# Transformer block on one core: the front part in turns of four max products and six projection products, with every second max product in a transpose bank

## The chip, the cores and the metric

The kernel runs on one core of a Trainium2 chip. The metric is the device time of one execution in microseconds (us), taken as the median over runs. The engines have short names here: PE is TensorE (PEld its weight loads), DVE is VectorE, ACT is ScalarE, POOL is GpSimd, SP is SyncE, which here only issues DMAs. Every engine works through its own queue in order. Where one needs what another makes, a semaphore holds it back, and everything behind it in its queue.

## The reference

One transformer block with modulation from a condition vector c, for 2048 rows of 512 numbers, in float32. The attention has 32 heads of size 16 that share one key and one value head.

```
sa, ca, ga, sb, cb, gb = silu(c) @ w_mod            # six rows of 512
h = layernorm(x) * (1 + ca) + sa
q, k, v = h @ wq, h @ wk, h @ wv                     # q: 32 heads x 16, k and v: one head of 16
p = softmax(q @ k.T / 4)                             # 32 heads, 2048 x 2048 each
x = x + ga * ((p @ v) @ wo)
h = layernorm(x) * (1 + cb) + sb
x = x + gb * (gelu(h @ w1 + b1) @ w2 + b2)           # 1376 hidden
```

## The kernel before

**Tiling.** The projections run in float32 precision: each operand is split in a high and a low part, and each product is three (`mm3`, L155 and after). Attention is cut into 64 units, each of 256 rows and four heads. A unit goes through two passes over the keys. The first makes scores only for their row maxima: *max products* `m` (PE, L512, 64 rows of the array, 512 keys each), of each of which DVE takes the maximum (L517, tile `mx`). With the maxima of a unit complete, `put_max` (L536) reduces them further (DVE, L565 and L566), POOL turns them into two rows, a high and a low part (`mt`, `mh`, `ml`), and `send` (L550) writes these into the query tile `qst` by DMA. Unit 0's four DMAs are issued half by SP and half by ACT. The second pass makes the scores again, now less their maximum (products `e`, L617), ACT takes the exps (L621), and PE multiplies them with the values (`acc`, L638).

**The front part.** Before the unit loop, the program normalises x in four blocks of 512 rows. For each block, `turn1` transposes it (tiles `tp`), `mod1` applies scale and shift (ACT, `h`, and its split `bigH`, `bigL`), and `kv_products` makes keys and values in `kps`: twelve products in four groups of three. From these, `kv_out` copies the high part of the keys into `ks` and the values into `vt` (ACT), `low_k` writes the low part (DVE), and `repeat_k` copies it to the other half of the array (ACT). `v_out` transposes the values (`vps`) and ACT copies them out (`va`, L420). Four groups of three query products (`qps`, "q 1") and the rows of the late modulation (`modl`, eight products at a time) come here too.

**Order.** The order is written by hand. `SLOTS` (L25) lists entries: a number of max products, then named jobs. The loop at L1353 goes through it; `chunk` makes the max products, alternately for the two halves of the array. After the list, the loop at L1376 makes max products up to a fixed count (two more), and `keep_warm` (L286) issues `WARM[3]` products on weights, whose result nobody reads (`idle`), in bank e2. Then the unit loop begins with its first `e`.

**Banks.** PE writes into PSUM banks. Max products turn through three (tag m), and a product waits until the reduce of the third product before it has read its bank. Three more, e0 to e2, are handed out in turn by `ebank()` to the transposes of the front part, and belong to the `e` products later. The projections have two others (x, v).

Of the kernel before, what the change touches and what calls it, by code (L numbers as in the profile page):

```python
# [8 lines left out]
F32 = mybir.dt.float32  # L9
F32R = mybir.dt.float32r  # L10
AF = mybir.ActivationFunctionType
ALU = mybir.AluOpType
AX = mybir.AxisListType

P = 128
# [7 lines left out]
LEAD_0 = 6  # L23
FIRST_MAX = ((0, 0), (1, 0), (0, 1), (1, 1), (0, 2), (0, 3), (1, 2), (1, 3))
SLOTS = ((2, "keys 1", "keys 1"), (2, "keys 1", "keys 1"), (2, "low 1", "heads 2"), (2, "heads 2", "k 1"), (1, "warm"), (1, "heads 2"), (2, "heads 2", "v 0"),  # L25
# [4 lines left out]
MAX_WAIT = (1, 4)  # L30
QBUFS = 4
PREP = 4
# [9 lines left out]
SOON = 6  # L42
GROUP = 4
NORM_WAIT = 6
WARM = (4, 16, 2, 5)
MOD_WAIT = 3
AHEAD = 4.5

# [1 line left out]
def raw(ap):  # L50
    return ap.bitcast(F32)
# [3 lines left out]
def adaln_mqa_mlp(  # L55
# [15 lines left out]
    nc = tc.nc  # L71
    _, S, D = x.shape
# [4 lines left out]
    BQ = 512  # L77
# [35 lines left out]
    ks = const.tile([P, S], F32R, name="ks")  # L113
# [13 lines left out]
    def ebank():  # L127
        turns[0] += 1
        return dict(tag=f"e{turns[0] % 3}", bufs=1)
# [30 lines left out]
    def mm3(ps, pairs, every=0, cost=0, begin=True, end=True):  # L160

        n, last = 0, 3 * len(pairs) - 1
        for wh, wl, xh, xl in pairs:
            for a, b_ in ((wh, xh), (wl, xh), (wh, xl)):
                nc.tensor.matmul(ps, a, b_, start=begin and n == 0, stop=end and n == last)  # L165
                n += 1
                if every and n % every == 0:
                    yield cost
# [50 lines left out]
    pro = pro_ctx.enter_context(tc.tile_pool(name="pro", bufs=1))  # L219
# [66 lines left out]
    def keep_warm(n, **place):  # L286

        for k in range(n):
            if k == 0 or not place:
                ps = psum.tile([P, BQ], F32, name=f"idle{len(idles)}", **(place or dict(tag="m", bufs=3)))  # L290
                idles.append(ps)
            nc.tensor.matmul(ps, wkH[:, 0, :], wkH.rearrange("p k n -> p (k n)"), start=True, stop=True)
# [64 lines left out]
    def stats1(b, between=None):  # L357
        mv, rs = ln_stats(xts[b], pro, QT, between)
        nm = pro.tile([P, QT], F32, name=f"nm{b}", tag="nm", bufs=2)
        if b:  # L360
            nc.gpsimd.tensor_tensor(out=nm, in0=mv[:, :, 0], in1=rs, op=ALU.mult)
            nc.gpsimd.tensor_scalar(out=nm, in0=nm, scalar1=-1.0, scalar2=0.0, op0=ALU.mult, op1=ALU.add)
        hts_stats[b] = mv, rs, nm

    def xhat1(b, eng):

        mv, rs, nm = hts_stats[b]
        xt = xts[b]
        for t in range(QT):
            if eng is nc.scalar:  # L370
                nc.scalar.activation(xt[:, t, :], xt[:, t, :], AF.Identity, scale=rs[:, t:t + 1], bias=nm[:, t:t + 1])
            else:
                eng.tensor_scalar(out=xt[:, t, :], in0=xt[:, t, :], scalar1=mv[:, t, 0:1], scalar2=rs[:, t:t + 1],
                                  op0=ALU.subtract, op1=ALU.mult)
            yield

    def turn1(b, d):
        ps = psum.tile([P, BQ], F32, name=f"tp{b}_{d}", **ebank())
        for t in range(QT):
            nc.tensor.transpose(ps[:, t * P:(t + 1) * P], xts[b][:, t, d * P:(d + 1) * P], ident)  # L380
        tps[b, d] = ps

    def mod1(b, d, eng_h, eng_l, between=None):
        hH, hL = hts[b]
        h32 = pro.tile([P, BQ], F32, name=f"h32_{b}_{d}", tag="h32", bufs=4)
        nc.scalar.activation(h32, tps.pop((b, d)), AF.Identity, scale=ca1[:, d:d + 1], bias=sa[:, d:d + 1])
        split(hH[:, d, :], hL[:, d, :], h32, eng_h, eng_l, between)

    kps = {}

    def kv_products(b):
        hH, hL = hts[b]
        kps[b] = psum.tile([P, BQ], F32, name=f"kps{b}", tag="x" if b == 3 else "v")
        return mm3(kps[b], [(wkH[:, k, :], wkL[:, k, :], hH[:, k, :], hL[:, k, :]) for k in range(KD)], 3)

    def kv_out(b):
        ps = kps[b]
        cols = slice(b * BQ, (b + 1) * BQ)
        vt = pro.tile([P, BQ], F32, name=f"vt{b}", tag="vt", bufs=2)
        for r in range(2):  # L400
            nc.scalar.copy(ks[64 * r:64 * r + 48, cols], ps[64 * r:64 * r + 48, :])
        nc.scalar.copy(vt[32:64, :], ps[32:64, :])
        vts[b] = vt

    def low_k(b):
        cols = slice(b * BQ, (b + 1) * BQ)
        nc.vector.tensor_tensor(out=ks[32:48, cols], in0=kps.pop(b)[32:48, :], in1=raw(ks[32:48, cols]), op=ALU.subtract)

    def repeat_k(b):
        cols = slice(b * BQ, (b + 1) * BQ)  # L410
        nc.scalar.copy(ks[96:112, cols], raw(ks[32:48, cols]))

    vts = {}

# [821 lines left out]
    first = [sum(size[:u]) for u in range(NU + 1)]  # L1236
    mp = Max()

    def chunk(n):
        for _ in range(n):  # L1240
            mp.step(mp.done % 2)

    act, dve, pool = nc.scalar, nc.vector, nc.gpsimd

    def k_products(b):
        for _ in kv_products(b):
            pass

    draining[0] = True
    late = [qproj_late(b, g) for b in range(2) for g in range(KD)]  # L1250
# [10 lines left out]
    def run(job, n=99):  # L1261
        for _ in range(n):
            if next(job, True):
                return

    def heads(b):

        for d in range(KD):
            turn1(b, d)
            mod1(b, d, pool if d == 1 else act, dve if b == 1 and d > 1 else pool)  # L1270
            if (b, d) == (2, KD - 1):
                load_mods(3)
            yield

    def keys(b):
        for i, _ in enumerate(kv_products(b)):
            if i == KD - 1:
                kv_out(b)
            yield

    def late_rows():
        for k in range(KD):
            if k == 0:
                mod_state["ps"] = psum.tile([P, D], F32, name="modl", tag="x")
            mod_rows(mod_state["ps"], k, mods_late[k])
            yield

    def q_group():
        for i in range(KD):
            next(projections[0])  # L1290
            if i == KD - 1:
                next(projections.pop(0))
            yield

    def warm():
        keep_warm(WARM[2], tag="x")
        yield

    def one(fn, *args):
        fn(*args)  # L1300
        yield
# [13 lines left out]
    turn1(0, 3)  # L1315
    keep_warm(WARM[0])
    mod1(0, 1, pool, dve, lambda: stats1(1))
# [3 lines left out]
    rows = xhat1(1, act)  # L1321
# [9 lines left out]
    run(rows)  # L1331
    run(keys(0))
    low_k(0)
    load_mods(0)
    load_mods(1)
    h1 = heads(1)
# [2 lines left out]
    def last_h(t):  # L1339
        if t == QT - 1:  # L1340
            run(h1)

    stats1(3, last_h)
    load_mods(2)
    repeat_k(0)
    run(xhat1(2, act))
    run(xhat1(3, pool))
    keep_warm(WARM[1])
    work = {"keys 1": keys(1), "heads 2": heads(2), "heads 3": heads(3), "q 1": q_group(), "keys 2": keys(2), "keys 3": keys(3),
            "v 0": one(v_out, 0), "v 1": one(v_out, 1), "v 2": one(v_out, 2), "v 3": one(v_out, 3), "rows": late_rows(),  # L1350
            "low 1": one(low_k, 1), "low 2": one(low_k, 2), "low 3": one(low_k, 3), "k 1": one(repeat_k, 1), "k 2": one(repeat_k, 2), "k 3": one(repeat_k, 3), "load": one(load_q, 2), "warm": warm(),
            "wq 1": one(prep_wq, 1), "wq 2": one(prep_wq, 2), "wq 3": one(prep_wq, 3)}
    for n, *names in SLOTS:  # L1353
        chunk(n)
        for name in names:
            next(work[name])
    assert 0 in placed and len(mods_late) == KD
    draining[0] = False
    nc.gpsimd.tensor_scalar(out=b1r, in0=b1c, scalar1=GELU_R, scalar2=0.0, op0=ALU.mult, op1=ALU.add)
# [16 lines left out]
    while mp.done < lead[0]:  # L1376
        chunk(1)
# [205 lines left out]
```

## Time and profile before

| | us |
|---|---|
| median of 3 runs | 1557.55 (1556.18 to 1559.13) |
| the profiled execution | 1555.99, span 1554.10 |
| heads-3 transposes end, projections of keys 2 begin on PE | 47.27 |
| L566 of unit 0 begins on DVE | 69.78 |
| first idle product | 73.75 |
| first `e` product | 75.14 |
| granted TensorE clock | 1.00 |

Rows of a timeline give start, duration, engine, line, operation, output and inputs, a count of like instructions in a row, and in brackets how long the engine stood before it and what ended this. Starts are counted from the span's beginning. Durations overlap on PE, whose products are pipelined, so what a product costs there is read from the distance of starts. Rows of the chain give start, length, engine and line. Rows by stretches give the stretch and its length, each engine's busy time, the granted clock and the DMA share.

### The profile page before, as it was taken

Reading aid. Unit: us, or ns where it says so; the run is one execution under the profiler, and the core shown is the slowest. Engines: PE = TensorE matmul, PEld = TensorE weight load, DVE = VectorE, ACT = ScalarE, POOL = GpSimd, SP = SyncE. Lnnn points to the kernel's source line nnn. Section 1 sums busy time; section 2 is a strip of 40 time slices with the busy share of each in tenths; the row PEclk is TensorE's granted clock in tenths of the full one; section 3 lists DMA queues with packets and bytes.
Section 4 is the critical chain, followed back from the end, with each engine's and each line's share of the span. In section 5 each row is a group of like instructions: output and inputs, shape, how many; then the busy total and the mean of one; then the engine's idle time right before and its main releaser. Section 6 shows DMA issues by size and latency. Waiting matters only on the chain.

```text
span 1554.1 us, 41556 instructions
## 1 busy us (share of the span) xinstructions
PE 1537.9 (99%) x16405; PEld 954.4 (61%) x16405; DVE 1398.3 (90%) x2488; ACT 1230.4 (79%) x2401; POOL 683.7 (44%) x1206
## 2 busy tenths in 40 slices
PE   7999999999999999999999999999999999999999
PEld 4455555567655665557655676556655676566658
DVE  7999999999999999999999999999999999999814
ACT  5577778788877887788877888788877888778874
POOL 5535432867422571246521563235711574046511
PEclk9999999999999999999999999999999999999999
DMA  7226412413030220303112120302212230203141
GB/s 240 102 89 199 151 57 81 130 51 97 18 105 26 72 68 28 103 19 109 33 51 79 56 87 16 111 26 88 68 30 73 60 101 25 87 28 99 48 150 48
DMA packets 84215, 120.85 MB, mean 78 GB/s; under 512 B 21342, under 2 KB 57438, under 8 KB 83764
## 3 DMA queue, kind: packets, MB, share of 16 engines
q1 hardware_dynamic: 84004, 118.18, 23.7%
q8 instruction: 130, 2.13, 0.6%
q14 instruction: 65, 0.53, 0.1%
q10 hardware_dynamic: 16, 0.00, 0.0%
HBM read 90.87 MB, written 26.74 MB: 76 GB/s over the span
## 4 chain that ended last, share of the span: by engine, by line
PE 86%; DVE 8%; issue 3%; POOL 2%; DMA 1%; ACT 0%; SPq 0%; POOLq 0%; DVEq 0%
PE acc L638 29%; PE m L512 23%; PE e L617 16%; PE w1ps L198 8%; DVE mx L517 6%; PE w2ps L198 2%; PE w2ps L188 2%; DMA xt<-in_A_x_dram 1%; PE w1ps L188 1%; PE wops L198 1%; PE tp L198 1%; PE qps L198 1%; PE kps L165 1%; DVE st L823 0%; DVE x L816 0%
## 5 line engine op out<-in xcount | busy, mean ns | idle before, releaser
L517 DVE TENSOR_REDUCE mx<-m 128x1 f32<-128x512 f32 x2048 | 1270.6, 682 | 86.6 <-PE m L512 65.1
L621 ACT ACTIVATE p<-e 128x512 f32<-128x512 f32 x2048 | 1098.8, 598 | 255.1 <-PE e L617 112.0
L512 PE MATMUL m<-ks,qst 64*128 64x512 f32 x2048 | 836.7, 429 | 2.0 <-DVE mx L517 0.6
L617 PE MATMUL e<-qst,ks 64*128 64x512 f32 x2048 | 740.2, 412 | 0.0
L638 PE MATMUL acc<-p,va 128*32 128x256 f32 x8192 | 548.0, 385 | 0.0
L512 PEld LDWEIGHTS m<-ks,qst 64*128 64x128 f32 x2048 | 368.2, 184 | 205.1 <-DVE mx L517 173.5
L617 PEld LDWEIGHTS e<-qst,ks 64*128 64x128 f32 x2048 | 359.6, 184 | 89.3 <-ACT p L621 62.5
L638 PEld LDWEIGHTS acc<-p,va 128*32 128x32 f32 x8192 | 214.0, 109 | 213.9 <-issue 110.9
L198 PE MATMUL w1ps<-h2H,w1t 64*128 64x256 f32 x1232 | 235.5, 287 | 0.0
L560 POOL TENSOR_SCALAR mt<-turned 8x32 f32<-8x32 f32 x256 | 53.1, 208 | 399.9 <-DVE turned L566 387.9
L198 PEld LDWEIGHTS w1ps<-h2H,w1t 64*128 64x128 f32 x1232 | 186.0, 185 | 28.9 <-DVE mx L517 14.8
L198 PE MATMUL w1ps<-h2L,w1t 64*128 64x256 f32 x616 | 169.3, 275 | 0.0
L198 PE MATMUL w2ps<-w2H,gH 64*128 64x512 f32 x274 | 120.3, 439 | 0.0
L198 PEld LDWEIGHTS w1ps<-h2L,w1t 64*128 64x128 f32 x616 | 114.1, 185 | 0.0
L198 PE MATMUL w2ps<-w2L,gH 64*128 64x512 f32 x274 | 107.5, 392 | 0.0
L198 PE MATMUL w2ps<-w2H,gL 64*128 64x512 f32 x274 | 106.9, 390 | 0.0
L975 POOL TENSOR_SCALAR tt<-tt 128x256 f32<-128x256 f32 x77 | 31.0, 402 | 131.5 <-ACT tt L974 96.5
L140 POOL TENSOR_TENSOR gL<-z,gH 128x256 fp32r<-128x256 f32 x77 | 57.0, 741 | 6.4
L976 POOL TENSOR_TENSOR tt<-tt,z 128x256 f32<-128x256 f32 x77 | 56.7, 736 | 6.4
L986 POOL TENSOR_TENSOR z<-tt,z 128x256 f32<-128x256 f32 x77 | 56.4, 732 | 6.0
L985 POOL TENSOR_TENSOR tt<-tt,z 128x256 f32<-128x256 f32 x77 | 56.5, 733 | 0.0
L198 PEld LDWEIGHTS w2ps<-w2H,gH 64*128 64x128 f32 x274 | 50.4, 184 | 6.7 <-DVE ot L1038 2.5
(193 smaller groups left out, 1503.5 us busy)
## 6 DMA issues: line engine op xcount, KB each, us to landing
w1t<-dw SPq DMA_DIRECT2D x82, 512.0 KB
qst<-dq SPq DMA_DIRECT2D x384, 32.0 KB
do<-oc SPq DMA_DIRECT2D x62, 128.0 KB
dw<-w1s SPq DMA_DIRECT2D x11, 512.0 KB
xt<-in_A_x_dram SPq DMA_DIRECT2D x4, 1024.0 KB
dq<-qH SPq DMA_DIRECT2D x16, 256.0 KB
dq<-qL SPq DMA_DIRECT2D x16, 256.0 KB
x<-in_A_x_dram SPq DMA_DIRECT2D x8, 512.0 KB
```

Of the source, the lines that this page charges most:

```text
L140: eng_l.tensor_tensor(out=dst_l, in0=src, in1=raw(dst_h), op=ALU.subtract)
L188: nc.tensor.matmul(ps, a, b_, start=first_, stop=last_)
L198: ins = nc.tensor.matmul(ps, a[rows], b_[rows], start=first_ and s == 0, stop=last_ and s == 1)
L512: nc.tensor.matmul(m, qsts[u][rows, j, t * P:(t + 1) * P], ks[rows, kc * 512:(kc + 1) * 512], start=True, stop=True)
L517: nc.vector.tensor_reduce(out=self.mx[u][:, i, kc:kc + 1], in_=m, axis=AX.X, op=ALU.max)
L560: nc.gpsimd.tensor_scalar(out=mt[:, g:g + 32], in0=turned[g:g + 4 * T, :], scalar1=1.0, scalar2=0.0, op0=ALU.mult, op1=ALU.add)
L617: nc.tensor.matmul(e, ks[rows, kt * P:(kt + 1) * P], rhs, start=True, stop=True)
L621: ins = nc.scalar.activation(dst, e, AF.Exp, scale=0.25)
L638: ins = nc.tensor.matmul(accs[u][32 * cidx:32 * cidx + 32, :], va[:, kt, :], rhs, start=kt == 0, stop=kt == NKT - 1)
L976: nc.gpsimd.tensor_tensor(out=tt, in0=tt, in1=z, op=ALU.mult)
L985: nc.gpsimd.tensor_tensor(out=tt, in0=tt, in1=z, op=ALU.mult)
L986: nc.gpsimd.tensor_tensor(out=z, in0=tt, in1=z, op=ALU.add)
```

## The change

From the twelfth entry of `SLOTS` on, right behind the transposes of the heads-3 part, the same jobs stand in another rhythm: four max products and then two groups of projections, instead of two and one. The numbers of max products that were zero are gone, an entry may now have numbers in its middle, and the last two max products are an entry too. In these entries every second max product gets a bank from `ebank()` instead of the m banks. The copy of the values `vt` is taken out of `kv_out` and put behind `low_k` for block 0, behind `repeat_k` for the others (`keep_v`). And `WARM[3]` is 12 instead of 5.

```diff
-         (2, "heads 3"), (2, "heads 3"), (2, "heads 3"), (2, "heads 3"), (0, "keys 2"), (2, "keys 2"), (2, "keys 2"), (2, "keys 2"),
-         (2, "low 2", "k 2", "v 1", "wq 1"), (0, "keys 3"), (2, "keys 3"), (2, "keys 3"), (2, "keys 3"), (2, "low 3", "k 3"),
-         (0, "v 2"), (2, "q 1"), (2, "q 1"), (2, "q 1"),
-         (2, "q 1", "rows"), (2, "v 3", "wq 2"), (2, "rows"), (2, "rows"), (2, "rows", "wq 3", "load"))
+         (2, "heads 3"), (2, "heads 3"), (2, "heads 3"), (2, "heads 3"),
+         (4, "keys 2", "keys 2"), (4, "keys 2", "keys 2"), (2, "low 2", 2, "k 2", "keys 3", "keys 3", "v 1", "wq 1"), (4, "keys 3", "keys 3"),
+         (2, "low 3", 2, "k 3", "v 2", "q 1", "q 1"), (4, "q 1", "q 1"), (4, "v 3", "wq 2", "rows"),
+         (2, "rows"), (2, "rows", "wq 3"), (2, "rows", "load"), (2,))
+WIDE = 11
...
-WARM = (4, 16, 2, 5)
+WARM = (4, 16, 2, 12)
...
     def kv_out(b):
         ps = kps[b]
         cols = slice(b * BQ, (b + 1) * BQ)
-        vt = pro.tile([P, BQ], F32, name=f"vt{b}", tag="vt", bufs=2)
         for r in range(2):
             nc.scalar.copy(ks[64 * r:64 * r + 48, cols], ps[64 * r:64 * r + 48, :])
-        nc.scalar.copy(vt[32:64, :], ps[32:64, :])
-        vts[b] = vt
...
+    def keep_v(b):
+        vts[b] = pro.tile([P, BQ], F32, name=f"vt{b}", tag="vt", bufs=2)
+        nc.scalar.copy(vts[b][32:64, :], kps.pop(b)[32:64, :])
 
     def repeat_k(b):
         cols = slice(b * BQ, (b + 1) * BQ)
         nc.scalar.copy(ks[96:112, cols], raw(ks[32:48, cols]))
+        if b:
+            keep_v(b)
...
     def chunk(n):
         for _ in range(n):
-            mp.step(mp.done % 2)
+            mp.step(mp.done % 2, **(ebank() if wide[0] and mp.done % 2 else {}))
...
     low_k(0)
+    keep_v(0)
...
-    for n, *names in SLOTS:
-        chunk(n)
-        for name in names:
-            next(work[name])
+    for i, slot in enumerate(SLOTS):
+        wide[0] = i >= WIDE
+        for part in slot:
+            if isinstance(part, int):
+                chunk(part)
+            else:
+                next(work[part])
```

How the instructions stand in their engines' queues, before and now, at three places. A row gives its place in the engine's queue, the line, the operation, outputs and inputs, and the semaphores it waits for, named by the engine or DMA queue that raises them; the numbers behind the names only keep tiles apart, and in `m_j_t_k_s` the last is the half of the array. Line numbers after the change are larger by one to six.

ACT around block 0's keys, before:

```order
17 L401 CAST ks<-kps_360 48x512 [waits PE_49]
18 L401 CAST ks<-kps_360 48x512
19 L402 COPY vt_373<-kps_360 32x512
20 L386 ACTIVATE h_1_0_391<-tp_0_386,sa,ca_67 128x512 [waits PE_49]
21 L135 CAST bigH<-h_1_0_391 128x512 [waits Activation_49]
```

The same place now:

```order
17 L401 CAST ks<-kps_360 48x512 [waits PE_49]
18 L401 CAST ks<-kps_360 48x512
19 L409 COPY vt_376<-kps_360 32x512 [waits DVE_49]
20 L387 ACTIVATE h_1_0_391<-tp_0_386,sa,ca_67 128x512 [waits PE_49]
21 L136 CAST bigH<-h_1_0_391 128x512 [waits Activation_49]
```

The order of the rows is the same, but the copy of the values now waits for DVE (`low_k`), and `h` stands behind it.

ACT at the end of the front part, before; `qH` is the high part of the query projection, `va<-vps` the copy of the last block's transposed values, the DMAs are `send`'s for unit 0:

```order
61 L450 COPY q_0_1_787<-qps_1_754 128x512 [waits PE_49,Pool_49]
62 L135 CAST qH_1_785<-q_0_1_787 128x512 [waits Activation_49]
63 L420 COPY va<-vps_804 128x4x16 [waits PE_49]
64 L342 CAST wqH<-wqf 128x4x64 [waits DMAHW4_49]
65 L342 CAST wqH<-wqf 128x4x64
66 L555 DMA qst_157<-mh_824 1x4x128 [waits DMAHW7_49,PE_49,Pool_49]
67 L555 DMA qst_157<-ml_825 1x4x128 [waits DMAHW1_49,Pool_49]
```

And now:

```order
61 L454 COPY q_0_1_787<-qps_1_760 128x512 [waits PE_49,Pool_49]
62 L136 CAST qH_1_785<-q_0_1_787 128x512 [waits Activation_49]
63 L559 DMA qst_157<-mh_809 1x4x128 [waits DMAHW7_49,PE_49,Pool_49]
64 L559 DMA qst_157<-ml_810 1x4x128 [waits DMAHW1_49,Pool_49]
65 L424 COPY va<-vps_823 128x4x16 [waits PE_49]
66 L343 CAST wqH<-wqf 128x4x64 [waits DMAHW4_49]
67 L343 CAST wqH<-wqf 128x4x64 x3
```

The two DMAs, which wait for POOL, moved ahead of the copy `va` and of two casts.

PE ahead of the unit loop, before:

```order
198 L297 MATMUL modl<-wml_578,csb 32x512 [waits DMAHW4_49]
199 L297 MATMUL modl<-wml_578,csb 32x512 x3
200 L512 MATMUL m_1_0_2_0_879<-ks,qst_158 128x512 [waits DVE_49]
201 L512 MATMUL m_1_0_2_1_882<-ks,qst_158 128x512 [waits DVE_49]
202 L512 MATMUL m_1_1_2_0_885<-ks,qst_158 128x512 [waits DVE_49]
203 L512 MATMUL m_1_1_2_1_888<-ks,qst_158 128x512 [waits DVE_49]
204 L292 MATMUL idle_891<-wkH 128x512 [waits Activation_49]
205 L292 MATMUL idle_891<-wkH 128x512 x4
206 L617 MATMUL e_0_0_1_898<-qst_157,ks 128x512 [waits DMAHW7_49,DMAHW1_49]
```

And now:

```order
199 L516 MATMUL m_1_0_2_0_862<-ks,qst_158 128x512
200 L516 MATMUL m_1_0_2_1_865<-ks,qst_158 128x512 [waits Activation_49]
201 L298 MATMUL modl<-wml_578,csb 32x512 [waits DMAHW4_49]
202 L298 MATMUL modl<-wml_578,csb 32x512 x3
203 L516 MATMUL m_1_1_2_0_878<-ks,qst_158 128x512 [waits DVE_49]
204 L516 MATMUL m_1_1_2_1_881<-ks,qst_158 128x512 [waits DVE_49]
205 L293 MATMUL idle_891<-wkH 128x512 [waits DVE_49]
206 L293 MATMUL idle_891<-wkH 128x512 x11
207 L621 MATMUL e_0_0_1_905<-qst_157,ks 128x512 [waits DMAHW7_49,DMAHW1_49]
```

The last `modl` products now stand between the last two pairs of max products. The second product of the first of these pairs waits for ACT (its bank held `vps_823`), and the first idle product for DVE (its bank is that of the last max product) instead of ACT.

More of the change, by code (lines that the diff above doesn't have):

```diff
@@ L398, in kv_out @@
         cols = slice(b * BQ, (b + 1) * BQ)
-        vt = pro.tile([P, BQ], F32, name=f"vt{b}", tag="vt", bufs=2)
         for r in range(2):
             nc.scalar.copy(ks[64 * r:64 * r + 48, cols], ps[64 * r:64 * r + 48, :])
-        nc.scalar.copy(vt[32:64, :], ps[32:64, :])
-        vts[b] = vt
     def low_k(b):
         cols = slice(b * BQ, (b + 1) * BQ)
-        nc.vector.tensor_tensor(out=ks[32:48, cols], in0=kps.pop(b)[32:48, :], in1=raw(ks[32:48, cols]), op=ALU.subtract)
+        nc.vector.tensor_tensor(out=ks[32:48, cols], in0=kps[b][32:48, :], in1=raw(ks[32:48, cols]), op=ALU.subtract)
+    def keep_v(b):
+        vts[b] = pro.tile([P, BQ], F32, name=f"vt{b}", tag="vt", bufs=2)
+        nc.scalar.copy(vts[b][32:64, :], kps.pop(b)[32:64, :])
     def repeat_k(b):
@@ L1237, in adaln_mqa_mlp @@
     mp = Max()
+    wide = [False]
     def chunk(n):
         for _ in range(n):
-            mp.step(mp.done % 2)
+            mp.step(mp.done % 2, **(ebank() if wide[0] and mp.done % 2 else {}))
     act, dve, pool = nc.scalar, nc.vector, nc.gpsimd
-    def k_products(b):
-        for _ in kv_products(b):
-            pass
     draining[0] = True
```

## The prediction

> **What bounds the kernel now.** I read the engine shares and the ended chain of the page, then busy time by stretches, to see what a microsecond of the front part is worth later.
>
> ```profile
> PE 1537.9 (99%) x16405; PEld 954.4 (61%) x16405; DVE 1398.3 (90%) x2488; ACT 1230.4 (79%) x2401; POOL 683.7 (44%) x1206
> PE 86%; DVE 8%; issue 3%; POOL 2%; DMA 1%; ACT 0%; SPq 0%; POOLq 0%; DVEq 0%
> 47.50:75.14 27.64, 27.04 (x122) 12.29 (x120) 25.13 (x42) 11.31 (x23) 13.62 (x20) 1.00 0.06 22
> 80.00:1280.00 1200.00, 1199.22 (x13287) 741.67 (x13289) 1125.90 (x1972) 978.60 (x1905) 541.67 (x956) 1.00 0.24 74
> ```
>
> The unit loop begins with the first `e` product; from 80 us on PE is busy 1199.22 of 1200 us. The loop has no slack in which a late start could be made up, and its order is the same in both kernels, so I read the change from one time: when does the first `e` start? Before the loop, in 47.50 to 75.14, DVE (25.13 busy) stands almost as high as PE (27.04). The timelines of both, and the chain, show who waits:
>
> ```profile
> 43.30 4.87 DVE L517 TENSOR_REDUCE mx<-m 128x1 f32<-128x512 f32 x8 [0.16 <-PE m L512]
> 48.68 5.27 DVE L517 TENSOR_REDUCE mx<-m 128x1 f32<-128x512 f32 x8 [0.51 <-PE m L512]
> 54.04 0.68 DVE L407 TENSOR_TENSOR ks<-kps,ks 16x512 fp32r<-16x512 f32 x1
> 54.76 5.21 DVE L517 TENSOR_REDUCE mx<-m 128x1 f32<-128x512 f32 x8
> 67.05 2.48 DVE L517 TENSOR_REDUCE mx<-m 128x1 f32<-128x512 f32 x4 [1.05 <-PE m L512]
> 69.56 0.19 DVE L565 TENSOR_REDUCE mm<-mx 128x8 f32<-128x32 f32 x1
> 69.78 0.21 DVE L566 STREAM_TRANSPOSE turned<-mm 128x32 f32<-128x32 f32 x1
> ...
> 33.30 1.60 PE kps L165 x6
> 48.64 0.90 PE kps L165 x3
> 65.58 1.00 PE modl L297 x8
> 72.59 0.69 DVE mx L517
> 73.32 0.50 PE m L512
> ...
> 47.48 0.78 ACT L386 ACTIVATE h<-tp,sa,ca 128x512 f32<-128x512 f32 x1 [0.46 <-POOL bigL L140]
> ...
> 48.15 0.50 PE L512 MATMUL m<-ks,qst 64*128 64x512 f32 x2
> 48.58 0.51 PE L165 MATMUL kps<-bigH,wkH 128*128 128x512 f32 x1
> 73.75 1.47 PE L292 MATMUL idle<-wkH 128*128 128x512 f32 x5
> 75.14 0.49 PE L617 MATMUL e<-qst,ks 64*128 64x512 f32 x2
> ```
>
> A reduce takes 0.69 us, and eight that never wait take 4.87: one each 0.60 us. A pair of max products takes PE 0.43 (48.15 to 48.58), and DVE starts 0.53 behind its product (48.15, 48.68). DVE waited 0.51 and 1.05 us for PE, and its eights took 5.27 and 5.21: this stretch swings between both engines. At its end the last max product waited for a reduce (72.59, then 73.32), five idle products ran from 73.75, and the first `e` came at 75.14.
>
> **The change, part by part.** I number the max products from the heads-3 part's end 1 to 36; 28 completes unit 0's row maxima. Times are on the axis of before.
>
> *Six projection products in turn.* Three take PE 0.90, six 1.60, so 0.20 goes with each return to them. Per four max products PE needs 0.66 + 1.60 (a pair costs 0.43, and two products more some 0.23) instead of 2 × (0.43 + 0.90): 2.26 against 2.66. Four reduces take DVE 2.40. So DVE becomes the slower one here, and of the saving only what DVE had waited comes through. Product 1 now stands ahead of the projections; DVE starts on it at 48.08, one pitch behind the eight that began at 43.30, instead of 48.68. To the last of the 28 there are 27 pitches (16.20) and two `low_k` (1.78: 0.89 each beyond the pitch, from 54.04 and 54.76), and three waits that I find by playing the order through: 0.37 at product 5, because product 4 waits for the ACT copy out of a transpose bank until 48.26 (the row at 47.48) and six projections follow; 0.28 each at 17 and 25, because 16 and 24 wait for the banks of 12 and 20 ahead of six more. Reduce 28 starts at 66.99. In before L566 ended at 69.99, and from 67.05 its four reduces began, so the last began at 68.85 and L566 ended 1.15 later; now it ends at 68.14: **-1.85**. The six-bank ring brings nothing beyond this where DVE is the slower.
>
> *The V copy behind `low_k`.* For block 0 the order on ACT was two casts, the V copy, then `h`; DVE's `low_k` waited for the V copy. Now the V copy waits for `low_k`, with `h` behind it:
>
> ```profile
> 25.01 1.16 ACT L401 CAST ks<-kps 48x512 fp32r<-48x512 f32 x2
> 26.18 0.58 ACT L402 COPY vt<-kps 32x512 f32<-32x512 f32 x1
> 26.79 0.78 ACT L386 ACTIVATE h<-tp,sa,ca 128x512 f32<-128x512 f32 x1
> 26.79 0.68 DVE L407 TENSOR_TENSOR ks<-kps,ks 16x512 fp32r<-16x512 f32 x1 [0.71 <-ACT vt L402]
> 31.58 1.07 DVE L140 TENSOR_TENSOR bigL<-h,bigH 128x512 fp32r<-128x512 f32 x1 [0.64 <-ACT bigH L135]
> 32.97 0.17 DVE L212 TENSOR_SCALAR ve<-mv 128x4 f32<-128x4 f32 x1
> 33.22 1.01 POOL L214 TENSOR_TENSOR rs<-ve,mhalf 128x4 f32<-128x4 f32 x1 [1.12 <-DVE ve L212]
> 34.76 8.26 POOL L373 TENSOR_SCALAR xt<-xt,mv,rs 128x512 f32<-128x512 f32 x4
> 43.20 0.66 PE L380 MATMUL tp<-ident,xt 128*128 128x128 f32 x4
> ```
>
> `low_k` runs 26.21 to 26.89, the copy to 27.51, `h` at 27.54 instead of 26.79: 0.75 later. Behind `h` stands a chain that waits at each step: ACT's `bigH`, DVE's `bigL` (31.58), `ve`, POOL's `rs` (33.22) and its four `xt` (34.76 to 43.02), and the heads-3 transposes on PE (43.20), which feed the front part. I take it whole: **+0.75**; L566 ends at 68.89. The bounds are 0 (swallowed by DVE's stream) and 0.75. For blocks 1 to 3 the move takes 0.58 us of ACT out of `low_k`'s way where ACT is waiting for PE anyway: nothing.
>
> *The late transposes in the way of product 34.* Product 34 now takes the bank of the last V transposes, which ACT copies out (`va`, L420). In before this copy ran at 67.41, ahead of two DMAs that ACT issues for unit 0's maxima; now products 25 to 28 stand earlier than the transposes, and in ACT's order the two DMAs come first. They wait for L566 and for POOL's work behind it, and everything behind them on ACT waits too:
>
> ```profile
> 67.41 0.21 ACT L420 COPY va<-vps 128x64 f32<-128x64 f32 x1 [0.50 <-PE vps L419]
> 71.51 1.35 ACTq L555 DMA_DIRECT2D qst<-mh  x1
> 72.96 0.59 ACTq L555 DMA_DIRECT2D qst<-ml  x1
> 73.59 0.74 ACT L342 CAST wqH<-wqf 128x256 fp32r<-128x256 f32 x2 [5.35 <-issue]
> 71.56 0.45 POOL L140 TENSOR_TENSOR ml<-mt,mh 8x128 fp32r<-8x128 f32 x1
> ```
>
> ACT stood until 73.59, 3.60 behind L566's end. So `va` starts at 68.89 + 3.60 = 72.49, ends at 72.70, and product 34 starts at 72.73, over two microseconds after PE was ready for it. What is queued behind it on PE: the last eight `modl` products, 35, 36, the idle ones and every `e`. ACT's own queue behind the DMAs (the `wqH` casts, then the copy of `modl`) has until the first exp and hides.
>
> *The idle products wait for the last reduce, and are twelve.* They stand in bank e2. In before this bank's last reader was an ACT copy long done; now it is product 36's, so the first idle product waits for reduce 36. From 34: 0.43 + 1.00 of `modl` bring 35 at 74.16; reduce 36 starts 0.53 + 0.60 behind and takes 0.69: 75.98, and the first idle product starts at 76.02. Five took 1.39 from start to `e` (73.75, 75.14); seven more at 0.2275 (below) make 2.98: `e` at 79.0. The DMAs of the maxima have landed long before.
>
> ```profile
> 28.27 3.64 PE idle L292 x16
> ```
>
> Sixteen in 3.64 give the 0.2275.
>
> **Sum.** 79.0 against 75.14: +3.9. Of this the idle products are +1.6, their wait behind 34 and reduce 36 +3.4, and -1.1 is what is left of the front's gain after the V copy. The profiled execution took 1555.99 us (span 1554.10), 1.56 under the median of 1557.55; +3.9 makes it 1559.9, and a median of 1561.4.
>
> The Trainium skill (TensorEngine Tiling (Array Packing), Key Properties) says that changing the tiling mode drains TensorE. The 0.20 us per turn agree, max products having 64 rows and projections 128; by that rule alone, on a PE that never waits, six times 0.40 (2.66 less 2.26) would be saved, 2.4 us, and after the 1.6 of idle products the change would gain 0.8.
>
> **Rivals.**
>
> *The gain comes through (the other side).* PE's saving of six times 0.40 shows at the loop's start, if ACT never blocks product 34 and the reduces never pause. It can go no further than DVE: 48.08 + 35 × 0.597 (4.87 less 0.69, over seven) + 1.78 + 0.48 (what L565 and L566 add) + 0.69 puts reduce 36's end and the first idle product at 71.9 even so, and `e` at 74.9: -0.2, 1557.3. For it speaks that DVE waited 1.05 at one place; against it that the idle products then must wait for DVE's whole stream. It decides for faster only if the V copy's 0.75 is swallowed as well; and even then by less than a measurement can tell.
>
> *The block at 34 is not there.* If ACT's copy is not held by the DMAs, or they issue sooner, the replay gives an idle start at 73.0, `e` at 76.0, with the V copy's shift 76.7: +0.9 to +1.6, so 1558.4 to 1559.1. For it: the 1.35 of the first DMA issue may hold a wait of that run. Against it: ACT's row says 5.35 of standing.
>
> *PE slows down behind the gaps.* PE now stands about 2 us ahead of 34 and 1.4 ahead of the idle products.
>
> ```profile
> 8.34 5.17 PE L297 MATMUL modr<-wm,csb 128*32 128x512 f32 x16 [8.34 <-DMA wm<-in_w_mod_dram]
> 12.04 1.47 PE L297 MATMUL modr<-wm,csb 128*32 128x512 f32 x6
> 65.51 1.06 PE L297 MATMUL modl<-wml,csb 128*32 128x512 f32 x8
> 27.61 0.66 PE L380 MATMUL tp<-ident,xt 128*128 128x128 f32 x4 [1.25 <-ACT h L386]
> ```
>
> After 8.34 us without work the same kind of product took 0.245 (six in 1.47), later 0.133 (eight in 1.06): 1.85 times as long. If such a slow stretch as long as 8.34 to 13.44 fell on the idle products and the first `e`s, 5.1 × (1 - 1/1.85) = 2.3 us would be lost: +6.2, 1563.8. Against it: after 1.25 us of standing the transposes took 0.66, the same as at 43.20, and the granted clock is 1.00 in every stretch. The Trainium skill (TensorE: Matmul & The Clock Gate, Part 1) says that TensorE falls to half its clock after an idle window of about 3.4 us; neither gap is that long, and by that rule the time stays at the forecast unless both count as one.
>
> **How the numbers follow.** Forecast 0.55 (its own range 1560.2 to 1562.6: the V copy's 0.75 and half a microsecond each way in the replay and the medians); gain comes through 0.08; no block at 34 0.22; PE slow 0.10; dearer in another way 0.05. A measurement of this kernel tells about 0.2% from no change, 3.1 us: same reaches to 1560.7. Same: 0.22, 0.05 of the gain, and 0.13 of the forecast's lower side, 0.40; faster 0.03; slower 0.42 + 0.15 = 0.57. The range goes from 1557.8, leaving out only the gain, to 1564.5.
>
> **What would show it.** Right: L566 ends about 1.1 us earlier than 69.99; ACT's `va` of the last V transposes right behind both DMA issues; a PE gap of some 2 us ahead of product 34, released by ACT; idle products behind DVE's last reduce at about 76; `e` near 79; block 0's V copy behind `low_k` and the transposes of 43.20 up to 0.75 later. Wrong: product 34 released by DVE, idle products by about 74, or products behind the gaps at nearly double length.

## The result and the profile after

The changed kernel took 1563.71 us (median; 1563.19 to 1565.21), the kernel before 1556.91 us in the same comparison (1555.39 to 1559.13): a ratio of 1.0045, 95% interval 1.0032 to 1.0058. That is +6.8 us where +3.9 was forecast; 1563.7 lies in the range (1557.8 to 1564.5), above the forecast's own 1560.2 to 1562.6.

The profiled execution took 1564.87 us, its span is 1563.10. First its stretches; the number before the last two of a row is the granted clock of TensorE, which was 1.00 everywhere in before:

```profile
24.00:38.00 14.00, 11.96 (x52) 8.62 (x50) 9.94 (x24) 10.92 (x17) 9.04 (x11) 0.88 0.38 118
...
70.00:76.00 6.00, 3.94 (x19) 0.85 (x12) 2.65 (x5) 1.46 (x5) 3.56 (x7) 0.76 0.12 24
76.00:80.00 4.00, 2.62 (x8) 1.96 (x7) 1.29 (x2) 0.00 (x0) 0.32 (x2) 0.50 0.05 15
80.00:84.00 4.00, 4.00 (x13) 2.54 (x13) 0.10 (x1) 0.87 (x2) 0.00 (x0) 0.58 0.00 0
84.00:90.00 6.00, 5.90 (x47) 3.15 (x49) 6.00 (x11) 4.95 (x11) 0.00 (x0) 1.00 0.01 3
```

PE's clock fell to half in two places, at the start of the front part and ahead of the loop. The timeline of PE shows what stands in front of each:

```profile
28.32 0.77 PE L381 MATMUL tp<-ident,xt 128*128 128x128 f32 x4 [1.99 <-ACT h L387]
28.74 5.51 PE L293 MATMUL idle<-wkH 128*128 128x512 f32 x16
...
72.93 0.66 PE L516 MATMUL m<-ks,qst 64*128 64x512 f32 x1 [2.06 <-ACT va L424]
73.52 1.94 PE L298 MATMUL modl<-wml,csb 128*32 128x512 f32 x8
75.39 0.79 PE L516 MATMUL m<-ks,qst 64*128 64x512 f32 x2
77.56 5.49 PE L293 MATMUL idle<-wkH 128*128 128x512 f32 x12 [1.38 <-DVE mx L521]
82.98 0.65 PE L621 MATMUL e<-qst,ks 64*128 64x512 f32 x2
...
86.88 1.07 PE L642 MATMUL acc<-p,va 128*32 128x256 f32 x16
```

In before, the sixteen idle products at 28 us were these:

```profile
28.03 3.89 PE L292 MATMUL idle<-wkH 128*128 128x512 f32 x16
```

Now they took 5.51 us, behind a stand of 1.99 us. Product 34 came at 72.93, released by ACT's copy `va`; the eight `modl` products behind it took 1.94 instead of 1.06, the twelve idle ones 5.49, and the first `e` came at 82.98, 7.84 us later than in before. ACT and DVE at the same places:

```profile
26.89 0.58 ACT L409 COPY vt<-kps 32x512 f32<-32x512 f32 x1 [0.75 <-DVE ks L405]
70.51 1.43 ACTq L559 DMA_DIRECT2D qst<-mh  x1
72.04 0.59 ACTq L559 DMA_DIRECT2D qst<-ml  x1
72.67 0.21 ACT L424 COPY va<-vps 128x64 f32<-128x64 f32 x1 [5.76 <-DMA qst<-mh]
...
44.63 10.86 DVE L521 TENSOR_REDUCE mx<-m 128x1 f32<-128x512 f32 x18 [0.17 <-PE m L516]
68.78 0.21 DVE L570 STREAM_TRANSPOSE turned<-mm 128x32 f32<-128x32 f32 x1
76.22 1.29 DVE L521 TENSOR_REDUCE mx<-m 128x1 f32<-128x512 f32 x2 [1.89 <-PE m L516]
```

The V copy waited 0.75 for `low_k`, `va` stands behind both DMAs, and the first idle product stands behind the last reduce (76.22, two in 1.29). DVE now ran eighteen reduces without a stop, where it had waited 0.51 in before, and L566 of unit 0 began at 68.78. From the first `e` on the shift is passed on: the last L566 began at 1474.8 in before and at 1483.2 now, 8.4 later; the spans differ by 9.0. The profiled execution was 1.2 us over its own median and before's 0.9 under its own, so the medians differ by less than the two profiles do.

### The profile page after: what moved, and what is told of

Same layout as the page of the kernel before. It is cut to its first block, busy times and chain, and to the rows that moved or that the text cites. A ratio compares the mean times of both kernels' runs of the same rounds, so it can differ in the third digit from the quotient of the medians.

```text
span 1563.1 us, 41561 instructions
## 1 busy us (share of the span) xinstructions
PE 1543.0 (99%) x16412; PEld 957.8 (61%) x16412; DVE 1397.9 (89%) x2488; ACT 1230.2 (79%) x2401; POOL 683.8 (44%) x1206
## 4 chain that ended last, share of the span: by engine, by line
PE 85%; DVE 9%; issue 3%; POOL 2%; DMA 1%; ACT 0%; ACTq 0%; SPq 0%; POOLq 0%; DVEq 0%
PE acc L642 29%; PE m L516 23%; PE e L621 16%; PE w1ps L199 8%; DVE mx L521 7%; PE w2ps L199 2%; PE w2ps L189 2%; PE w1ps L189 1%; DMA xt<-in_A_x_dram 1%; PE wops L199 1%; PE qps L199 1%; PE tp L199 1%; PE idle L293 1%; DVE st L827 0%; DVE x L820 0%
```

## The experiments

Twelve kernels, in three groups of four, each group with the kernel before on its own chip; each ratio is against those runs. The profiles' axes begin up to half a microsecond before or behind that of before, so the table counts from one event that no edit touches, the first ACT cast of block 0's keys (L401, at 25.01 in before): how much later than in before L566 of unit 0 began, and the first `e`. These two columns come from one profiled execution of each kernel, which can lie some way from its median (1.2 us over it in the changed kernel and e6, 1.3 to 1.5 under it in e2, e5 and e8), so `e` and the time can't be expected to agree more closely than that.

| kernel | L566 | first `e` | median, us | ratio to before, interval |
|---|---|---|---|---|
| changed | -0.96 | +7.88 | 1563.71 | 1.0045, 1.0032 to 1.0058 |
| e1 fill ahead of 34 | -1.02 | +4.20 | 1560.72 | 1.0032, 1.0019 to 1.0045 |
| e2 V transposes early | -0.60 | +2.01 | 1559.54 | 1.0019, 1.0011 to 1.0028 |
| e3 V copy first | -1.92 | +5.56 | 1561.29 | 1.0035, 1.0021 to 1.0049 |
| e4 five idle | -0.95 | +4.39 | 1560.46 | 1.0029, 1.0018 to 1.0040 |
| e5 three edits | -1.57 | -0.35 | 1557.32 | 0.9999, 0.9991 to 1.0008 |
| e6 idle in v | -1.58 | -1.42 | 1554.72 | 0.9988, 0.9979 to 0.9997 |
| e7 before, V copy behind | +0.16 | +0.13 | 1557.97 | 1.0012, 1.0003 to 1.0021 |
| e8 three banks | +1.65 | +3.75 | 1561.45 | 1.0028, 1.0018 to 1.0037 |
| e9 ten in v | -1.56 | -1.35 | 1555.16 | 0.9991, 0.9982 to 1.0000 |
| e10 both fills | -1.19 | +4.01 | 1560.63 | 1.0029, 1.0018 to 1.0040 |
| e11 banks alone | -1.92 | -0.91 | 1556.80 | 1.0001, 0.9992 to 1.0010 |
| e12 banks, ten in v | -2.03 | -1.84 | 1554.87 | 0.9992, 0.9983 to 1.0001 |

### e1: PE kept busy ahead of product 34

```diff
-         (2, "rows"), (2, "rows", "wq 3"), (2, "rows", "load"), (2,))
+         (2, "rows"), (2, "rows", "wq 3"), (1, "fill", 1, "rows", "load"), (2,))
...
+    def fill():
+        keep_warm(9, tag="v")
+        yield
```

> The changed kernel with nine more idle products on PE ahead of product 34, in the free bank v, where PE stood 2.06 us for ACT. No wait is taken away: 34 still comes when ACT has copied the transposes, at 72.9. Theory (PE slows down because it stood before 34 and again before the idle products): filled, the last modl products take 1.06 again and not 1.94, the twelve idle products 2.99 and not 5.49, e comes near 79.3 instead of 82.98, and the time is 3 to 4 us under that of the change, about 1560. Rival (the waits alone make the loss, the slow products have another cause): 34, the idle products and e stay where they are, 1563.7, or later by what of the nine reaches past 72.9.

PE of this kernel:

```profile
70.54 2.36 PE L293 MATMUL idle<-wkH 128*128 128x512 f32 x9
72.82 0.50 PE L516 MATMUL m<-ks,qst 64*128 64x512 f32 x1
73.25 1.06 PE L298 MATMUL modl<-wml,csb 128*32 128x512 f32 x8
...
76.12 3.04 PE L293 MATMUL idle<-wkH 128*128 128x512 f32 x12 [1.38 <-DVE mx L521]
79.09 0.51 PE L621 MATMUL e<-qst,ks 64*128 64x512 f32 x2
```

Product 34 came where it came before (72.82), and what follows ran at full pace: `modl` 1.06, twelve idle products 3.04, `e` at 79.09. Nothing was taken away but PE's standing still. So in these two profiles the slow products are the price of the stand ahead of 34, about 3.7 us at `e`. The wait itself, the wait for reduce 36 (1.38 us are left of it) and the seven more idle products make the rest. The times alone would not have told it: e1 is 5.1 us over before and the changed kernel 6.8, and their intervals overlap. Two of e1's five executions (1561.69 and 1562.02) still had a mean clock of 0.997; no trace shows where.

### e2: the V transposes one step earlier

```diff
-(4, "v 3", "wq 2", "rows"),
+("v 3", 4, "wq 2", "rows"),
```

> The changed kernel with the last V transposes one step earlier, ahead of products 25 to 28, so that ACT copies them out before it stops for the two DMAs. Theory (34 waited for that copy): no wait of PE for ACT at 34, products 35 and 36 near 72, reduce 36 done at 73.9, and PE warm, since only one gap of some 1.4 us is left: idle products 73.9 to 76.9, e 6 us earlier than in the change, 1557.7, within 1 us of before. Rival (the wait for reduce 36 and the twelve idle products make the most of it): e at 78 or later, 1559 or more. Rival (the clock has to do with the earlier part, from 26 us on): idle products slow again, e at 79 or later.

ACT and PE of this kernel:

```profile
66.72 0.21 ACT L424 COPY va<-vps 128x64 f32<-128x64 f32 x1
...
71.70 0.49 PE L516 MATMUL m<-ks,qst 64*128 64x512 f32 x2
74.07 3.02 PE L293 MATMUL idle<-wkH 128*128 128x512 f32 x12 [1.88 <-DVE mx L521]
77.02 0.51 PE L621 MATMUL e<-qst,ks 64*128 64x512 f32 x2
```

The copy runs at 66.72, ahead of the DMAs, and PE no longer waits for ACT: 35 and 36 came at 71.70, and the idle products began as reduce 36 ended, at 74.07. `e` at 77.02 is within 0.1 of what was expected. One place in a list takes 5.9 us off `e`. It has a price too: L566 is 0.36 later than in the changed kernel, since the transposes now stand ahead of products 25 to 28 and DVE waits 0.59 us for product 25, not 0.21. The time fell by 4.2 of the expected 6: 1559.5, not 1557.7; the profiled execution, at 1558.24, was one of the faster ones.

### e3: block 0's V copy ahead of low_k

```diff
     low_k(0)
-    keep_v(0)
...
+    keep_v(0)
     low_k(0)
```

(and `keep_v` leaves `kps` in place for `low_k`)

> The changed kernel with block 0's V copy ahead of low_k again, as before the change; the other blocks as changed. Theory (the copy behind low_k lengthened PE's gap ahead of the last heads-1 transposes from 1.25 to 1.99 us, and the sixteen idle products behind it were slow, 5.16 instead of 3.64): gap 1.25, sixteen in 3.64, first max product near 31.9, the stream of eighteen reduces from 43.3 instead of 44.63, e 1.3 us earlier than in the change, 1562.4. Rival (a shift of 0.75 only, the slow sixteen are chance): 1563.0, with the sixteen slow in this run too or fast in both.

PE of this kernel:

```profile
27.31 0.66 PE L381 MATMUL tp<-ident,xt 128*128 128x128 f32 x4 [1.25 <-ACT h L387]
27.72 3.88 PE L293 MATMUL idle<-wkH 128*128 128x512 f32 x16
...
72.12 1.31 PE L298 MATMUL modl<-wml,csb 128*32 128x512 f32 x8
...
75.54 4.91 PE L293 MATMUL idle<-wkH 128*128 128x512 f32 x12 [1.38 <-DVE mx L521]
80.39 0.50 PE L621 MATMUL e<-qst,ks 64*128 64x512 f32 x2
```

The stand is 1.25 again and the sixteen are fast; L566 is 0.96 earlier than in the changed kernel, 1.92 earlier than in before. `e` came 2.3 us earlier than in the changed kernel, more than the 1.3 expected, because the second slow stretch was shorter (`modl` in 1.31, not 1.94, and twelve in 4.91, not 5.49). Whether the early slow stretch has a price of its own at `e`, e10 tells.

### e4: five idle products

```diff
-WARM = (4, 16, 2, 12)
+WARM = (4, 16, 2, 5)
```

> The changed kernel with five idle products ahead of the loop instead of twelve. Theory (they run at half pace here, 0.45 us each): e 3.2 us earlier after the same wait, but the first e and max products are slow in their place for what the stretch of slow PE still has to last, so between 1.6 and 3.2 us are won, 1560.5 to 1562.1. Rival (the idle products shorten the slow stretch, as they are there for): 1563 or more.

PE of this kernel:

```profile
77.00 2.50 PE L293 MATMUL idle<-wkH 128*128 128x512 f32 x5 [1.38 <-DVE mx L521]
79.43 0.79 PE L621 MATMUL e<-qst,ks 64*128 64x512 f32 x2
```

Five idle products took 2.43 us to `e`, 0.49 each, against 0.45 each for the twelve: at half pace, seven of them are worth 3.2 us, twice the 1.6 of the forecast, and the time fell by about as much (3.3 by the medians, 2.5 by the ratios). The seven more did not make the slow stretch any shorter.

### e5: the three edits together

e2, e3 and e4 in one kernel.

> The changed kernel with three edits at once: the last V transposes ahead of products 25 to 28, block 0's V copy ahead of low_k, five idle products instead of twelve. What is left is the new rhythm, the six banks, and the wait of the idle products for reduce 36. Theory (the three cost all of the loss, and the front's gain is real): L566 starts near 67.9 instead of 69.78 in before, reduce 36 ends at 72.8, idle products from 72.9, e at 74.2 to 74.3, 0.9 us ahead of before, 1555.8 against 1556.7. Rival (the new rhythm itself loses): e at 76 or later, 1558 or more.

PE of this kernel:

```profile
73.27 1.63 PE L293 MATMUL idle<-wkH 128*128 128x512 f32 x5 [1.88 <-DVE mx L521]
74.83 0.79 PE L621 MATMUL e<-qst,ks 64*128 64x512 f32 x2
```

The three edits take away the loss: no difference from before can be told any more (0.9999). L566 is 1.57 earlier than in before, but `e` only 0.35: PE stood 1.88 us for reduce 36, and the products behind it were slow again (the granted clock is 0.78 from 76 to 80). The front's gain is there, and it goes into the idle products' wait.

### e6: the idle products in a bank that is free

```diff
-    keep_warm(WARM[3], tag="e2", bufs=1)
+    keep_warm(WARM[3], tag="v")
```

on top of e5.

> As the three edits together, and the idle products in the free bank v instead of e2, so that they do not wait for reduce 36. Theory: they start right behind product 36 on PE, at 71.0, and end at 72.4; the maxima of unit 0 land some 4.3 us behind L566, at 72.3; e at 72.4 to 72.6, 2.6 us ahead of before, 1554. The third e now waits for reduce 36 at 72.9, which costs nothing. Rival (what DVE still has to do comes first): the first max products of the loop and the exps wait, acc begins no earlier than with the idle products in e2, and the time is that of the three edits alone.

PE and DVE of this kernel:

```profile
70.99 1.43 PE L293 MATMUL idle<-wkH 128*128 128x512 f32 x5
73.44 0.61 PE L621 MATMUL e<-qst,ks 64*128 64x512 f32 x2 [1.02 <-DVE mx L521]
...
77.44 1.93 PE L642 MATMUL acc<-p,va 128*32 128x256 f32 x16
...
68.06 4.83 DVE L521 TENSOR_REDUCE mx<-m 128x1 f32<-128x512 f32 x8
```

The idle products followed product 36 at once, and `e` came 1.42 earlier than in before, 1.1 earlier than in e5; 1554.72 and an interval that ends at 0.9997 make it the first kernel that is faster than before. The expected 72.4 to 72.6 was a microsecond too early: `e` waited 1.02 us. The trace puts this down to DVE, but reduce 36 had ended at 72.89, 0.55 us before `e` began, and by its queue row the first `e` waits for two DMA queues. It begins 5.52 us behind L566 here, 5.57 in e9 and 5.55 in e12. This points to the landing of unit 0's maxima, which the expectation had put at 4.3 behind L566; no row shows the landing itself. The products that followed were slow (sixteen `acc` in 1.93, where e9 and e12 have 1.07).

### e7: the V copy alone, on the kernel before

```diff
     low_k(0)
+    keep_v(0)
```

(with `keep_v` as in the change, for block 0 only; the other blocks copy in `kv_out` as before)

> The kernel before with one thing of the change alone: block 0's V copy behind low_k. Theory (it lengthens PE's gap at 26 us from 1.25 to 1.99, and PE then runs at half pace through most of sixteen idle products): sixteen in 5.1 to 5.5 instead of 3.64, the first max product at 34.1 instead of 31.84, everything to the loop 1.3 later, e at 76.4, 1 to 1.4 us over before. Rival (later waits swallow it): e at 75.1 to 75.5, no difference.

PE of this kernel:

```profile
28.81 0.66 PE L380 MATMUL tp<-ident,xt 128*128 128x128 f32 x4 [1.99 <-ACT h L386]
29.22 3.89 PE L292 MATMUL idle<-wkH 128*128 128x512 f32 x16
```

The theory missed: the stand of 1.99 us came, the sixteen idle products were fast all the same, and of the 0.75 only 0.13 arrived at `e` (75.73). Over eleven executions the kernel was still 0.12% slower: four took 1560.95 to 1561.07 at a mean clock of 0.996 or 0.997, the others 1556.97 to 1558.12 at 0.999 or 1.00. The profile is of one of the others, so where PE was slow in these four isn't shown. Their clock lacks about 5 us (0.003 to 0.004 of 1559), while the slow stretch at 28 us in the changed kernel lacks 1.7 (0.12 of 14), so they were slow for longer than that or at a second place too. The kernel before has this as well, in two of the 31 executions run beside e7 (1559.69 and 1560.29, 0.997 and 0.998).

### e8: three banks

```diff
-WIDE = 11
+WIDE = 99
```

> The changed kernel with all max products in the three m banks, as before the change; the rhythm, the V copy and the twelve idle products as changed. With three banks, the fourth max product of a turn waits for the reduce of the first, 1.26 us behind it, and six projections take 1.60 and the product 0.43 more: a turn takes 3.3 us instead of DVE's 2.4. Theory: DVE waits 0.8 to 0.9 in each of some seven turns, L566 is 5 to 6 us later than in the change, at 74; product 34 waits for DVE, not ACT; the idle products wait for ACT's copy behind the two DMAs, near 78; e at 81 to 83, 1562 to 1564. Rival (the banks matter little because DVE is the slower one either way): L566 within 2 us of the change, and, with no block at 34, e at 78 to 79, 1560.

DVE and PE of this kernel:

```profile
51.73 2.48 DVE L521 TENSOR_REDUCE mx<-m 128x1 f32<-128x512 f32 x4 [0.80 <-PE m L516]
71.66 0.21 DVE L570 STREAM_TRANSPOSE turned<-mm 128x32 f32<-128x32 f32 x1
...
79.12 0.51 PE L621 MATMUL e<-qst,ks 64*128 64x512 f32 x2
```

DVE waits 0.80 at the start of a turn, as expected, but not everywhere: L566 is 2.6 later than in the changed kernel, half of what the theory said and more than its rival, and 1.65 later than in before. The turns of four and six, together with the V copy behind `low_k`, lose when the banks are missing. `e` came earlier than the theory had it: PE reached the idle products at 76.15, just behind ACT's copy (75.76), and no product was slow; the granted clock is 1.00 in every stretch of this profile, which is of the fastest of nine executions (1559.99, median 1561.45).

### e9: ten idle products in bank v

e6 with `WARM = (4, 16, 2, 10)`.

> The kernel with the three edits and the idle products in bank v, with ten idle products instead of five, so that PE works from product 36 until the first e. Theory (the slow stretch from 76 us in the kernel with five came from PE's stand of 1.02 us ahead of e, and made some of its runs slower): ten from 71.0 end at 73.3, e stays at 73.4 to 73.6, the products behind it are at full pace, acc begins near 77.2 in every run, and the median is at the faster runs of the kernel with five, 1554.5, with no run over 1555.2. Rival (the slow stretch has nothing to do with that stand): some runs stay 1.3 us slower, granted clock under 1 behind e.

PE of this kernel:

```profile
70.99 2.55 PE L293 MATMUL idle<-wkH 128*128 128x512 f32 x10
73.47 0.57 PE L621 MATMUL e<-qst,ks 64*128 64x512 f32 x2
...
77.20 1.07 PE L642 MATMUL acc<-p,va 128*32 128x256 f32 x16
```

PE did not stand, `e` came at the same 73.47, the sixteen `acc` began at 77.20 and took 1.07, and all eleven executions had a mean clock of 1.00. That fits the stand of 1.02 us as the cause of e6's slow stretch, but doesn't show it: in e6 only two of the eleven executions had a mean clock under 1.00. The time, 1555.16, was not under that of e6, and the interval ends at 1.0000. Four executions took 1555.5 to 1555.9 at full clock, where none over 1555.2 was expected; what spreads them isn't shown.

### e10: both stands filled

e1, and nine idle products in bank x ahead of the last two blocks of heads-1 transposes:

```diff
         if t == QT - 1:
+            keep_warm(9, tag="x")
             run(h1)
```

> The changed kernel with both of PE's long stands filled with idle products: nine ahead of product 34, and nine in bank x ahead of the last but one heads-1 transposes at 26 us. No wait of the change is taken away, only PE's clock. Theory: the sixteen idle products take 3.64 and not 5.16, the first max product comes at 32.8, e at 78.0 to 78.4, granted clock 1.00 in every stretch and every run: the change's price without slow products, which is the forecast's sum, 1559.5 to 1560.3 against 1556.7. Rival (the early slow stretch is not from the stand): sixteen slow again, 1560.7 as with one fill.

PE and DVE of this kernel:

```profile
29.07 3.90 PE L293 MATMUL idle<-wkH 128*128 128x512 f32 x16
51.91 3.68 DVE L521 TENSOR_REDUCE mx<-m 128x1 f32<-128x512 f32 x6 [0.91 <-PE m L516]
...
76.52 3.00 PE L293 MATMUL idle<-wkH 128*128 128x512 f32 x12 [1.38 <-DVE mx L521]
79.45 0.51 PE L621 MATMUL e<-qst,ks 64*128 64x512 f32 x2
```

The sixteen are fast (3.90), and `e` is 4.01 later than in before, where the forecast's sum said 3.86 and the expectation 2.9 to 3.3. The time is 4.5 us over before's 1556.08, a ratio of 1.0029 where e1 has 1.0032. So the early slow stretch costs 0.2 us at `e`: with the sixteen fast, the first max product comes 1.6 us sooner than in e1, but DVE then waits 0.91 us for PE at 51.91, where in e1 and in the changed kernel it takes eighteen reduces without a stop.

### e11: the banks alone

On the kernel before:

```diff
-            mp.step(mp.done % 2)
+            mp.step(mp.done % 2, **(ebank() if wide[0] and mp.done % 2 else {}))
...
-    for n, *names in SLOTS:
+    for i, (n, *names) in enumerate(SLOTS):
+        wide[0] = i >= 11
```

> The kernel before with one part of the change alone: from the keys-2 part on, every second max product in a transpose bank. Turns of two and three, V copies and five idle products as before. Theory (the waits for banks cost PE some 2.6 us in before, and the last V transposes keep their place ahead of the DMAs here): PE goes through its turns without waiting, 1.33 per pair against DVE's 1.2; L566 starts at 68.2 to 68.8 instead of 69.78, the idle products wait for reduce 36 as in the change, 72.4, and e comes at 73.8 to 74.3, 1 us ahead of before: 1555.5. Rival (the banks bring nothing without the longer turns): e at 75 or later.

DVE and PE of this kernel:

```profile
54.31 4.87 DVE L517 TENSOR_REDUCE mx<-m 128x1 f32<-128x512 f32 x8
67.81 0.21 DVE L566 STREAM_TRANSPOSE turned<-mm 128x32 f32<-128x32 f32 x1
...
72.83 1.43 PE L292 MATMUL idle<-wkH 128*128 128x512 f32 x5 [2.50 <-DVE mx L517]
74.18 0.80 PE L617 MATMUL e<-qst,ks 64*128 64x512 f32 x2
```

With six banks and the old turns DVE takes eight reduces in 4.87, without a wait, and L566 begins 1.92 earlier than in before, as early as in e3 with the long turns. The banks make the front's gain, the turns of four and six add nothing to it. And again it is lost in the idle products' wait for reduce 36 (2.50 us) and the slow stretch behind: no difference in time.

### e12: the banks, and ten idle products in bank v

e11 with `WARM = (4, 16, 2, 10)` and the idle products in bank v.

> The same with ten idle products in bank v: the idle products no longer wait for reduce 36. Theory: product 36 ends on PE near 71, the idle products fill to 73.3, e at 73.3 to 73.6 behind reduce 36 and the landing of the maxima, 1.6 us ahead of before, 1554.9, the same as with the turns of four and six: then the longer turns bring nothing that the banks do not. Rival (the longer turns matter): e at 74 or later.

PE of this kernel:

```profile
73.80 0.59 PE L617 MATMUL e<-qst,ks 64*128 64x512 f32 x2 [0.53 <-DVE mx L517]
```

`e` is 1.84 earlier than in before, the earliest of all, as is L566 (-2.03). The time is that of e6 and e9 within their intervals: 0.08% under before, and as the interval reaches 1.0001, not shown to be faster. The banks and the idle products' new place reach without the long turns what e6 and e9 reach with them.

## Why the prediction was right, and where it fell short

**Six projections in turn, -1.85 at L566.** Measured where the V copy does not disturb it: -1.92 (e3). The size is right and the reason given for it was wrong, so that the two agree is in part luck. The prediction said that the six-bank ring brings nothing beyond what a slower DVE allows and put the gain down to the turns; the runs show the ring alone at -1.92 (e11), and the turns without it at +1.65 (e8, which holds the V copy's shift too). That DVE becomes the slower engine was right: it waits for PE at products 17 and 25 (0.20 and 0.21, at 60.12 and 66.04; 0.28 forecast), and at product 5 in e3 and e10 (0.58 and 0.91; 0.37 forecast), though not in the changed kernel, whose stream began late.

**The V copy, +0.75.** Between e3 and e10, which differ at that place by the V copy and a fill, L566 moved by 0.73. Between e3 and the changed kernel, where the sixteen were slow as well, it moved by 0.96. On the old turns almost all was swallowed (e7, 0.16).

**The block at product 34.** As forecast, step by step: `va` behind both DMAs (72.67, forecast 72.49), 34 released by ACT at 72.93 (72.73). e2 shows the cause by one moved entry.

**The idle products behind reduce 36, and seven more.** Right in kind; e6 against e5 prices the wait at 1.1 us at `e`. The seven were mis-sized in the changed kernel, since they ran at half pace: 3.2 us, not 1.6.

**The rival of a slow PE.** This is the step that failed: the sum had PE at full pace. The slow pace stood as a rival with 0.10, on the ground that 1.25 us of standing had not slowed PE and that the two gaps ahead of the loop would be only about 2 and 1.4 us. PE did slow down, both behind the gap ahead of 34 and at 28 us, where the prediction had gone by the 1.25 us of before although its own term lengthened that stand to 1.99. The other ground, a granted clock of 1.00 in every stretch, was weak: the stretch from 8 to 14 us in before reads 1.00 too, and the prediction's own slow products (0.245 each) lie in it. From product 34 to `e` the slow stretch cost 3.7 us: 0.9 in the `modl` products, 0.4 in 34 to 36, 2.4 in the twelve idle ones. The rival's time, 1563.8, is nearly what was measured, and that is luck: it came from a price of 2.3 us and a base of 1557.55, where the price was 3.7 at `e` and the base 1556.91. The result lies in the range only because the range was drawn up to this rival. With PE kept busy (e10) the change costs about the forecast's sum: `e` +4.01 for +3.86, and the time +4.5 (2.8 to 6.2 by its interval) for +3.9. Against the changed kernel's +6.8 the intervals still overlap, so it is the traces, and not the times, that show the slow pace as the rest.

The Trainium skill (TensorE: Matmul & The Clock Gate, Part 1) speaks of half the clock after an idle window of about 3.4 us. By that rule the forecast stood; here half pace followed stands of 1.0 to 2.5 us in some executions, so the measurement decides against reading the 3.4 us as a safe length of a single gap.

**The other rivals.** The gain that comes through (-0.2) did not come. e5 shows that it could not while the idle products wait for reduce 36: even without the block at 34 and with the V copy first they began at 73.27, where the rival had 71.9. A block that is not there would have given +0.9 to +1.6 at `e`; e2, which takes it away, gave +2.01.

## What to carry to other kernels

When a transfer or a copy moves ahead of something else in an engine's queue, look up what the things behind it release: here a DMA that waits for another engine, issued from ACT, stood ahead of the copy that frees a PSUM bank, and PE waited for the bank. A filler that keeps TensorE busy must stand in a bank and at a place that wait for nothing; one that waits for the last work of another engine is not there when it is needed, and its own length is then added to the path. Price a new stand of TensorE by what may run behind it at half pace, also where the stand is only one or two microseconds. And when a change joins a new rhythm with new banks, time each of the two alone: here the banks made the whole gain.

## What the runs showed of the hardware

The clock of TensorE falls after much shorter stands than expected, and not in each execution. Behind a stand of 1.25 us at the same place it stayed at 1.00 in the profiles of seven kernels; behind 1.99 us it fell in four of six profiles (slow in the changed kernel, e1, e2 and e4; not in e7 and e8). The shorter stand is no assurance: of the 77 executions of before beside the experiments, six had a mean clock of 0.997 or 0.998 and took 1558.76 to 1560.29, and no trace shows where they were slow. Ahead of the loop, 2.06 and 1.38 us with little work between were followed by 7 to 10 us at half pace (twice the length of a stretch times what its clock lacks to 1.00, over the stretches of the changed kernel, e3 and e4), 2.50 us in e11 by some 7, a single 1.88 us in e2 by none and in e5 by some 3.5, 1.02 us in e6 by some 3.5 (in the profile; nine of its eleven executions had a mean clock of 1.00), and 1.38 us in e1 and e10, where PE had been kept busy until then, by none. The slow pace was a factor of 1.8: `modl` 1.94 for 1.06, `acc` 1.93 for 1.07, an idle product of the twelve 0.45 for 0.25 (5.42 and, in e1, 2.97 from the first to `e`). What besides the stand's length decides it, these runs don't show.
